# Which of the first four blocks is convolved on TensorE, and on which queue the third block is loaded: a fused causal convolution and GELU feed-forward kernel

## The chip, the cores and the metric

The kernel runs on one core of a Trainium2 chip. The metric is the device time of one execution in microseconds; the time before is the median of seven executions. A core has TensorE (PE in the profile; its weight loads are PEld), VectorE (DVE), ScalarE (ACT), GpSimd (POOL) and SyncE (SP). SP, ACT and POOL can start DMAs. Those of SP and ACT go through hardware queues, those of POOL through a software ring.

## The reference

The input x has 8 sequences of 4096 tokens with 192 channels, in 8 heads of 24. Each head has seven weights, normalised by a softmax. A token's channel becomes the weighted sum of the same channel in this token and the six before it (zeros ahead of the sequence). Then comes a feed-forward layer.

```python
w = softmax(weight)                            # (8 heads, 7 taps)
x_pad = concatenate([zeros(B, 6, D), x], axis=1)
y[b, s, h, g] = sum_k w[h, k] * x_pad[b, s + k, h, g]
h = y.reshape(B * S, 192) @ w_in               # (32768, 2048)
g = 0.5 * h * (1 + erf(h / sqrt(2)))
out = g @ w_out                                # (32768, 192), float32
```

## The kernel before

The 32768 tokens are two halves that lie side by side on the partitions (64 channels of the first half on partitions 0 to 63, of the second on 64 to 127). Each half is cut into 34 blocks (`WS`): four of 256 tokens, blocks 0 to 3, then thirty of 512. The 192 channels are three groups of 64 (`NP = 3`, index `p`).

A block n goes through these stages:

- **Load** (`load`, L172 to L185): four DMAs into `xin[n % 3]`. Block 0 is shared by SP and ACT, block 1 by SP and POOL, all others are loaded by SP.
- **Transpose** (`trans`, L371, VectorE): 32x32 blocks from `xin` to `xT[n % 2]`, float32, channels on partitions. A tap of the convolution is then a shift by 32 columns; GpSimd fills in the columns that lie ahead of the block (`halo`, L253).
- **Convolution**, in one of two ways. Blocks with n < `ND` = 3: `xT` is cast to bf16 (`cast` on VectorE, for block 0 on ScalarE), TensorE multiplies by diagonal matrices of the taps (`pconv`, L537; 14 matmuls for each p) into a part of the output accumulators `ob`, and VectorE (`conv_out`, L366) or for block 0 ScalarE copies the result to `xc[n % 2]`. All later blocks: 21 VectorE operations (`conv`, L392; seven taps by three groups) accumulate in float32 and write `xc[n % 2]`.
- **First product** (`mm1`, L575): slices into the two buffers `hp`, eight slices for a block of 256 tokens, sixteen for one of 512. ScalarE applies GELU to a slice and writes `gT[n % 2]`.
- **Second product** (`mm2`, L603): for 128 tokens of each half (a group g; two or four groups in a block) 32 units of two matmuls, 16 in each of two phases that accumulate in the same bank, into `ob[group number % 2]`. TensorE does the second product of block n - 1 between the slices of the first product of block n: the units are dealt out to the slices (L643 to L656).
- **Eviction and store** (`evac`, L418; `store`): VectorE copies a group from `ob` to `osb`, and SP stores it.

Every engine works through its list in the order in which it is written, and semaphores carry the dependences. Three orders were written by hand:

- **VectorE** (L437 to L474): blocks 0 to 2 one by one. Then for each block from 3 on the 24 operations `ops0` (three transposes, 21 taps); between them, at the positions of the table `late`, the evictions. `(2, 1): (4, 23)` says that group 1 of block 2 is evicted ahead of operation 23 of block 4, its last tap.
- **TensorE**: `behind` (L570) puts the convolution parts of the next block behind slices of the present one: those of block 1 behind slices 2, 4, 6 of block 0, those of block 2 behind slices 1, 2, 3 of block 1. The units of block 0 are spread evenly over slices 2 to 7 of block 1, those of later blocks evenly over all slices.
- **Queues**: POOL issues W_in in three pieces (`win_in`), half of block 1's load, and W_out (L290; bf16 in the kernel, converted by the DMA). SP loads block 2 after the third piece of W_in has landed, block 3 after W_out has landed, and block 4 after block 3 has landed.

Of the kernel before, what the change touches and what calls it, by code (L numbers as in the profile page):

```python
# [11 lines left out]
def bass_lightweight_conv__then__act_gelu_exact_kernel(  # L12
# [21 lines left out]
    ND = 3  # L34
# [54 lines left out]
    with es:  # L89
# [15 lines left out]
        xTb = [sbt("xTb%d" % i, [128, NP * XB], BF16) for i in range(ND)]  # L105
# [12 lines left out]
        S_XG = sem("S_XG")  # L118
# [9 lines left out]
        S_CAST = [sem("S_CAST%d" % i) for i in range(ND)]  # L128
# [15 lines left out]
        CONVB = [  # L144
            [(ob[0], 0), (ob[0], 512), (ob[1], 0)],
            [(ob[0], 0), (ob[0], 512), (ob[1], 0)],
            [(ob[1], 0), (ob[1], 512), (ob[1], 256)],
        ]
# [6 lines left out]
        def cvd(n):  # L155

            return NCV * max(0, n - ND + 1)


        HC = [0]  # L160
        for n in range(NB):
            HC.append(HC[n] + (1 + NP if n < ND else 2))

# [4 lines left out]
        def xin_at(n):  # L168

            return 64 * (n // NX + 1) - (32 if n % NX == 1 else 0)  # L170
# [58 lines left out]
        def _(g):  # L229
# [21 lines left out]
            load(g, 1, (2, 3), S_XG)  # L251

            def halo(n):  # L253

                t, tw = (xTb[n], XB) if n < ND else (xT[n % 2], XW)
                dst = ap(t, 0, [[NP * tw, 128], [tw, NP], [32, HB]])
                if n >= ND + 2:
                    g.wait_ge(S_CV, cvd(n - 2))
                elif n >= 2:
                    g.wait_ge(S_PCE, NP * (n - 1))  # L260
# [12 lines left out]
                if n < ND:  # L273
                    for p in range(NP):
                        g.wait_ge(S_TR, NP * n + p + 1)
                        g.tensor_copy(  # L276
                            ap(t, p * tw + 1, [[NP * tw, 128], [32, HB], [1, 31]]),
                            ap(xT[n % 2], p * XW + WS[n], [[NP * XW, 128], [32, HB], [1, 31]]),
                        ).then_inc(S_HALO)
                    return  # L280
# [8 lines left out]
            win_in(FP[2], FP[3], S_WIN[2])  # L289
            g.dma_start(  # L290
# [7 lines left out]
        def _(v):  # L298
# [58 lines left out]
            def cast(n, p):  # L357
                v.wait_ge(S_TR, NP * n + p + 1)
                v.tensor_copy(  # L359
                    ap(xTb[n], p * XB + HL, [[NP * XB, 128], [1, WS[n]]]),  # L360
                    ap(xT[n % 2], p * XW + HL, [[NP * XW, 128], [1, WS[n]]]),
                ).then_inc(S_CAST[n])

            def conv_out(n, p):
                v.wait_ge(S_PC, NP * n + p + 1)
                b, o = CONVB[n][p]  # L366
                v.tensor_copy(  # L367
                    xc[n % 2][:, p * TB : p * TB + WS[n]], ap(b, o, [[1024, 128], [1, WS[n]]])
                ).then_inc(S_PCE)

            def trans(n, p):  # L371
                w = WS[n]
                if p == 0:
                    v.wait_ge(S_XIN[n % NX], xin_at(n))
                    if n == 1:
                        v.wait_ge(S_XG, 32)
                    if n >= ND + 2:
                        v.wait_ge(S_CV, cvd(n - 2))
                    elif n >= 2:
                        v.wait_ge(S_PCE, NP * (n - 1))  # L380
                    if n >= 1:
                        v.wait_ge(S_HALO, HC[n])
# [65 lines left out]
            dup(2)  # L448
            for p in range(NP):
                conv_out(1, p)  # L450
            for p in range(NP):
                trans(2, p)
            for p in range(NP):
                cast(2, p)
            for p in range(NP):
                conv_out(2, p)


            late = {(0, 0): (3, 9), (0, 1): (3, 16), (1, 0): (4, 1), (1, 1): (4, 9)}
            late.update({(2, 0): (4, 16), (2, 1): (4, 23), (3, 0): (5, 14), (3, 1): (6, 1)})  # L460
# [6 lines left out]
            order = sorted(late, key=lambda k: (late[k], k))  # L467
            for b in range(ND, NB):
                for o, op in enumerate(ops0):
                    while order and late[order[0]] <= (b, o):  # L470
                        evac(*order.pop(0))
                    run(b, op)
            for k in order:
                evac(*k)  # L474
# [57 lines left out]
        def _(t):  # L532
# [4 lines left out]
            def pconv(n, p, k):  # L537
# [3 lines left out]
                if k == KS - 1:  # L541
                    t.wait_ge(S_CAST[n], p + 1)
                    if n == 0:
                        t.wait_ge(S_DG, p + 1)
                    elif n == 2 and p == 0:
                        t.wait_ge(S_PCE, 2 * NP)
                    elif n == 2 and p == 2:
                        t.wait_ge(S_PCE, 2 * NP + 1)
                if k == KS - 2:
                    t.wait_ge(S_HALO, HC[n] + 2 + p)  # L550
                for hf in range(2):
# [6 lines left out]
                        xTb[n][r, x0 : x0 + w],  # L558
# [12 lines left out]
            for p in range(NP):  # L571
                for n, i in ((1, 2 + 2 * p), (2, 1 + p)):
                    behind[n - 1, i] = [(n, p, k) for k in range(KS - 1, -1, -1)]

            def mm1(n, i):  # L575
# [4 lines left out]
                if i == 0:  # L580
                    if n < ND:
                        t.wait_ge(S_PCE, NP * (n + 1))
# [20 lines left out]
            def mm2(m, g, ph, i):  # L603
# [4 lines left out]
                if i == 0:  # L608
                    if ph == 0:
                        if gg >= 2:  # L610
                            t.wait_ge(S_EV, gg - 1)
                        elif gg == 1:
                            t.wait_ge(S_PCE, NP * ND)
# [23 lines left out]

            def units(m):
# [4 lines left out]
            for n in range(NB):  # L643
                todo = units(n - 1) if n >= 1 else []
                for i in range(NSL[n]):
# [3 lines left out]

                    i0 = 2 if n == 1 else 0  # L650
                    a0 = len(todo) * max(0, i - i0) // (NSL[n] - i0)
                    a1 = len(todo) * max(0, i + 1 - i0) // (NSL[n] - i0)
                    if n == 1 and i == i0:
# [11 lines left out]
        def _(sp):  # L665
# [45 lines left out]
```

## Time and profile before

| | |
|---|---|
| median of 7 executions | 698.77 us (697.17 to 700.78) |
| the profiled execution: its own time | 699.72 us |
| the profiled execution: span of its trace | 697.7 us |
| TensorE busy | 687.5 us (99%) |
| VectorE busy | 553.2 us (79%) |
| ScalarE busy | 528.9 us (76%) |
| GpSimd busy | 40.8 us (6%) |
| mean granted TensorE clock | 0.996 |
| time from issue to landing: W_out | 12.5 us |
| the same, three of block 2's four DMAs (issued from 14 us on), median | 5.9 us |

The span runs from the first to the last instruction of the trace; the execution's own time also holds what lies around it, 2.0 us here. A time in the profile counts from the start of the span. A busy time is a sum over the whole span; whether an engine sets the pace in one stretch is read from what the others wait for there. In a line of a timeline the first number is the start, the second the length from the first to the end of the last of the merged instructions, and the bracket at the end is the idle time just before, with what ended it. The ends of matmuls are modelled and overlap the start of the next by some 0.2 us.

### The profile page before, as it was taken

How to read it: one execution, taken by the hardware profiler on the slowest of the kernel's cores; microseconds unless marked ns; L12 is line 12 of the kernel's file. 1: busy time of each engine (PE TensorE's matmuls, PEld its weight loads, DVE VectorE, ACT ScalarE, POOL GpSimd, SP SyncE). 2: the span in 40 equal slices, each digit the busy share in tenths (PEclk: the TensorE clock that was granted, in tenths of full speed). 3: DMA queues.
4: the chain of work that ended last, by engine and by line, in shares of the span. 5: the costliest groups of instructions: out<-in, count | busy, mean ns of one | idle time of the engine just before them, and what ended most of it. 6: DMA issues, size and time to landing. Idle time of an engine off the chain costs nothing.

```text
span 697.7 us, 25349 instructions
## 1 busy us (share of the span) xinstructions
PE 687.5 (99%) x11598; PEld 529.0 (76%) x11598; DVE 553.2 (79%) x915; ACT 528.9 (76%) x524; POOL 40.8 (6%) x89
## 2 busy tenths in 40 slices
PE   8899999999999999999999999999999999999997
PEld 5687777777777777777777777777777777777777
DVE  6499977898887897888897888897887898887811
ACT  6578877777777777777777777777777777777771
POOL 5100000000000000000000000000000000000000
PEclk9999999999999999999999999999999999999999
DMA  9768433455534455443455533455533455521013
GB/s 180 179 148 192 114 77 85 116 136 137 125 74 99 115 136 137 114 102 82 115 137 137 126 91 82 113 138 136 133 86 79 114 137 137 130 53 28 22 47 93
DMA packets 23083, 78.15 MB, mean 112 GB/s; under 512 B 6977, under 2 KB 11201, under 8 KB 19137
## 3 DMA queue, kind: packets, MB, share of 16 engines
q1 hardware_dynamic: 18832, 73.80, 44.5%
q0 software_dynamic: 3408, 1.96, 2.0%
q8 instruction: 91, 1.49, 1.0%
q10 hardware_dynamic: 736, 0.78, 0.4%
q14 instruction: 16, 0.12, 0.1%
HBM read 52.92 MB, written 25.17 MB: 112 GB/s over the span
## 4 chain that ended last, share of the span: by engine, by line
PE 94%; DVE 2%; DMA 2%; issue 0%; POOL 0%; SPq 0%; ACT 0%; DVEq 0%
PE ob L627 48%; PE hp L593 45%; DMA xin<-in_x_dram 2%; DVE acc L413 1%; DMA win<-in_moe_w_in_dram 1%; PE ob L555 1%; DVE xT L383 0%; DVE xc L413 0%; DVE acc L406 0%; POOL xTb L276 0%; SPq L178 0%; DVE osb L422 0%; ACT L479 0%; POOL win L232 0%; DVE xTb L359 0%
## 5 line engine op out<-in xcount | busy, mean ns | idle before, releaser
L522 ACT ACTIVATE gT<-hp 128x1024 bf16<-128x1024 f32 x512 | 523.3, 1024 | 150.3 <-PE hp L593 150.3
L627 PEld LDWEIGHTS ob<-wout,gT 64*128 64x128 bf16 x8192 | 368.7, 94 | 99.8 <-issue 1.1
L627 PE MATMUL ob<-wout,gT 64*128 64x192 bf16 x8192 | 428.6, 243 | 0.7 <-issue 0.6
L593 PE MATMUL hp<-xc,win 64*128 64x512 bf16 (+1 forms) x3264 | 423.8, 364 | 3.3 <-DVE xc L413 1.6
L413 DVE SCALAR_TENSOR_TENSOR acc<-xT,wcol,acc 128x512 f32<-128x512 f32 (+1 forms) x465 | 311.1, 731 | 0.0
L593 PEld LDWEIGHTS hp<-xc,win 64*128 64x128 bf16 x3264 | 166.4, 94 | 56.6 <-ACT gT L522 3.4
L422 DVE COPY osb<-ob 128x384 f32<-128x384 f32 x128 | 70.3, 549 | 125.8 <-PE ob L627 125.8
L383 DVE STREAM_TRANSPOSE xT<-xin 128x512 f32<-128x512 f32 (+1 forms) x102 | 61.2, 649 | 3.0 <-DMA xin<-in_x_dram 2.8
L413 DVE SCALAR_TENSOR_TENSOR xc<-xT,wcol,acc 128x512 bf16<-128x512 f32 (+1 forms) x93 | 63.3, 732 | 0.0
L282 POOL COPY xT<-xT 128x558 f32<-128x558 f32 x31 | 20.3, 654 | 591.4 <-DVE xT L383 591.4
L406 DVE TENSOR_SCALAR acc<-xT,wcol 128x512 f32<-128x512 f32 (+1 forms) x93 | 54.0, 633 | 1.1
L265 POOL COPY xT<-xT 128x18 f32<-128x18 f32 x28 | 11.2, 399 | 0.0
L555 PE MATMUL ob<-xTb,dg 64*64 64x256 bf16 x126 | 9.1, 292 | 1.3 <-DVE xTb L359 1.3
L555 PEld LDWEIGHTS ob<-xTb,dg 64*64 64x64 bf16 x126 | 6.8, 115 | 3.5 <-DVE xTb L359 1.8
L367 DVE CAST xc<-ob 128x256 bf16<-128x256 f32 x6 | 2.5, 421 | 8.8 <-PE ob L555 8.8
L535 PE MATMUL hp<-warm 128*128 128x512 bf16 x16 | 6.3, 578 | 1.3 <-DVE warm L299 1.3
L535 PEld LDWEIGHTS hp<-warm 128*128 128x128 bf16 x16 | 2.1, 139 | 4.9 <-issue 3.5
L344 DVE COPY win<-win 64x768 bf16<-64x768 bf16 (+1 forms) x6 | 4.1, 680 | 0.3
L276 POOL CAST xTb<-xT 128x186 bf16<-128x186 f32 x9 | 3.4, 386 | 11.3 <-DVE xT L383 11.3
L232 POOL DMA_DIRECT2D win<-in_moe_w_in_dram x6 | 3.9, 659 | 0.8 <-POOLq L696 0.8
L493 ACT ACTIVATE xTb<-xT 128x256 bf16<-128x256 f32 x3 | 1.1, 417 | 2.7 <-DVE xT L383 2.7
L501 ACT ACTIVATE xc<-ob 128x256 bf16<-128x256 f32 x3 | 1.2, 384 | 1.2 <-PE ob L555 1.2
(28 smaller groups left out, 14.0 us busy)
## 6 DMA issues: line engine op xcount, KB each, us to landing
xin<-in_x_dram SPq DMA_DIRECT2D x120, 380.0 KB, 6.7
out_dram<-osb SPq DMA_DIRECT2D x116, 192.0 KB, 3.1
xin<-in_x_dram SPq DMA_DIRECT2D x12, 188.0 KB, 3.9
out_dram<-osb SPq DMA_DIRECT2D x40, 48.0 KB, 1.9
wout<-in_moe_w_out_dram POOLq DMA_DIRECT2D x1, 768.0 KB, 12.5
win<-in_moe_w_in_dram POOLq DMA_DIRECT2D x4, 96.0 KB, 4.6
win<-in_moe_w_in_dram POOLq DMA_DIRECT2D x2, 192.0 KB, 4.5
out_dram<-osb ACTq DMA_DIRECT2D x8, 48.0 KB, 2.1
```

Of the source, the lines that this page charges most:

```text
L265: g.tensor_copy(dst, ap(xT[(n - 1) % 2], WS[n - 1] + 31, [[NP * XW, 128], [XW, NP], [32, HB]],),).then_inc(S_HALO)
L282: g.tensor_copy(ap(t, 1, [[NP * tw, 128], [tw, NP], [32, HB], [1, 31]]), ap(t, WS[n], [[NP * tw, 128], [tw, NP], [32, HB], [1, 31]]),).the ...
L344: v.tensor_copy(ap(win, 64 * (1 - hf) * NP * F + FH + FP[s], [[NP * F, 64], [F, NP], [1, FP[s + 1] - FP[s]]],), ap(win, 64 * hf * NP * F + ...
L383: v.transpose(ap(xT[n % 2], p * XW + HL, [[NP * XW, 128], [1, w]]), ap(xin[n % NX], 64 * p, [[TB // 32 * D, 128], [D, w // 32], [1, 32]],) ...
L406: ins = v.tensor_scalar(a, src, wk, None, ALU.mult)
L413: ins = v.scalar_tensor_tensor(dst, src, wk, a, op0=ALU.mult, op1=ALU.add)
L422: v.tensor_copy(ap(osb[m % 2], g * C, [[8 * C, 128], [4 * C, 2], [1, C]]), ap(ob[(G0[m] + g) % 2], 0, [[1024, 128], [512, 2], [1, C]]),).t ...
L522: a.activation(out=ap(gT[n % 2], i * c * 2 * w, dst), in_=ap(hp[u % 2], 0, src), func=AF.Gelu,).then_inc(S_GELU)
L535: t.matmul(hp[1][:, 0:512], warm[:, 0:128], warm[:, :])
L555: ins = t.matmul(b[r, o : o + w], dg[r, d0 : d0 + 64], xTb[n][r, x0 : x0 + w], start=(k == KS - 1), stop=(k == 0), tile_position=(64 * hf, ...
L593: ins = t.matmul(hp[u % 2][:, hf * TB + cc * w : hf * TB + cc * w + w], win[r, p * F + wcols(hf, f0) : p * F + wcols(hf, f0) + 128], xc[n ...
L627: ins = t.matmul(ob[gg % 2][:, 512 * sub : 512 * sub + C], gT[m % 2][r, c0 : c0 + 128], wout[r, CH[i] * C : (CH[i] + 1) * C], start=(ph == ...
```

## The change

Blocks 0, 1 and 3 are now the ones that are convolved on TensorE; the table `PC` gives the number of their bf16 tile, and `pce(n, p)` the count of `S_PCE` at which part p of block n is in `xc`. Block 2 goes through VectorE's 21 taps.

Block 2's load is issued by POOL, all four DMAs, behind the third piece of W_in and ahead of W_out, and has its own semaphore `S_XG[1]`. SP no longer loads block 2 and no longer waits for block 3's landing ahead of block 4.

VectorE's hand-written order now starts its 24 operations with block 2 and skips block 3, whose transposes, casts and conv_outs become entries of one list `side` with the evictions: block 1's conv_outs stand ahead of operations 1, 4 and 8 of block 2, block 3's transposes and casts ahead of block 4, its conv_outs ahead of operations 5, 7 and 9 of block 4. The evictions of blocks 0 to 3 have new places.

On TensorE the parts of block 3 stand behind slices 1, 2, 3 of block 2, in `ob[1]`. The units of block 0 are dealt to the slices of block 1 as 0, 0, 0, 11, 11, 10, 16, 16 and those of block 1 to block 2's as 7, 7, 6, 6, 6, 11, 11, 10.

```diff
     WS = [256] * 4 + [512] * ((HALF - 1024) // 512)
-    ND = 3
+    PC = {0: 0, 1: 1, 3: 2}
     NB = len(WS)
     OFF = [sum(WS[:n]) for n in range(NB)]
     assert sum(WS) == HALF
...
         block = es.enter_context(nc.Block())
-        CONVB = [
-            [(ob[0], 0), (ob[0], 512), (ob[1], 0)],
-            [(ob[0], 0), (ob[0], 512), (ob[1], 0)],
-            [(ob[1], 0), (ob[1], 512), (ob[1], 256)],
-        ]
+        CONVB = {
+            0: [(ob[0], 0), (ob[0], 512), (ob[1], 0)],
+            1: [(ob[0], 0), (ob[0], 512), (ob[1], 0)],
+            3: [(ob[1], 0), (ob[1], 512), (ob[1], 256)],
+        }
         NCV = NP * KS
         FQ = F // 8
...
         def cvd(n):
-            return NCV * max(0, n - ND + 1)
+            return NCV * sum(m not in PC for m in range(n + 1))
+
+        def pce(n, p):
+
+            return NP * PC[n] + p + 1
         HC = [0]
         for n in range(NB):
-            HC.append(HC[n] + (1 + NP if n < ND else 2))
+            HC.append(HC[n] + (1 + NP if n in PC else 2))
         def wcols(hf, f):
...
         def xin_at(n):
-            return 64 * (n // NX + 1) - (32 if n % NX == 1 else 0)
+            return 64 * (n // NX + 1) - (0, 32, 64)[n % NX]
         def load(e, n, qs=(0, 2, 1, 3), sm=None):
             mb = WS[n] // 32
...
                     channel_multiplier=1,
                 ).then_inc(S_IDN)
             win_in(FP[1], FP[2], S_WIN[1])
-            load(g, 1, (2, 3), S_XG)
+            load(g, 1, (2, 3), S_XG[0])
             def halo(n):
-                t, tw = (xTb[n], XB) if n < ND else (xT[n % 2], XW)
+                t, tw = (xTb[PC[n]], XB) if n in PC else (xT[n % 2], XW)
                 dst = ap(t, 0, [[NP * tw, 128], [tw, NP], [32, HB]])
-                if n >= ND + 2:
-                    g.wait_ge(S_CV, cvd(n - 2))
-                elif n >= 2:
-                    g.wait_ge(S_PCE, NP * (n - 1))
+                if n >= 2 and n not in PC:
+                    if n - 2 in PC:
+                        g.wait_ge(S_PCE, pce(n - 2, NP - 1))
+                    else:
+                        g.wait_ge(S_CV, cvd(n - 2))
                 if OFF[n] % SEQ == 0:
                     g.memset(dst, 0.0).then_inc(S_HALO)
                 else:
...
                             [[NP * XW, 128], [XW, NP], [32, HB]],
                         ),
                     ).then_inc(S_HALO)
-                if n < ND:
+                if n in PC:
                     for p in range(NP):
                         g.wait_ge(S_TR, NP * n + p + 1)
                         g.tensor_copy(
...
             g.wait_ge(S_IDN, 2)
             halo(0)
             win_in(FP[2], FP[3], S_WIN[2])
+            load(g, 2, (0, 2, 1, 3), S_XG[1])
             g.dma_start(
                 ap(wout, 0, [[NF * C, 128], [C, NF], [1, C]]),
                 ap(woutt, 0, [[C, 128], [128 * C, NF], [1, C]]),
...
             def cast(n, p):
                 v.wait_ge(S_TR, NP * n + p + 1)
                 v.tensor_copy(
-                    ap(xTb[n], p * XB + HL, [[NP * XB, 128], [1, WS[n]]]),
+                    ap(xTb[PC[n]], p * XB + HL, [[NP * XB, 128], [1, WS[n]]]),
                     ap(xT[n % 2], p * XW + HL, [[NP * XW, 128], [1, WS[n]]]),
-                ).then_inc(S_CAST[n])
+                ).then_inc(S_CAST[PC[n]])
             def conv_out(n, p):
-                v.wait_ge(S_PC, NP * n + p + 1)
+                v.wait_ge(S_PC, pce(n, p))
                 b, o = CONVB[n][p]
                 v.tensor_copy(
                     xc[n % 2][:, p * TB : p * TB + WS[n]], ap(b, o, [[1024, 128], [1, WS[n]]])
...
             def trans(n, p):
                 w = WS[n]
                 if p == 0:
-                    v.wait_ge(S_XIN[n % NX], xin_at(n))
-                    if n == 1:
-                        v.wait_ge(S_XG, 32)
-                    if n >= ND + 2:
+                    if xin_at(n) > 0:
+                        v.wait_ge(S_XIN[n % NX], xin_at(n))
+                    if n in (1, 2):
+                        v.wait_ge(S_XG[n - 1], 32 * n)
+                    if n >= 2 and n - 2 in PC:
+                        v.wait_ge(S_PCE, pce(n - 2, NP - 1))
+                    elif n >= 2:
                         v.wait_ge(S_CV, cvd(n - 2))
-                    elif n >= 2:
-                        v.wait_ge(S_PCE, NP * (n - 1))
                     if n >= 1:
                         v.wait_ge(S_HALO, HC[n])
                 v.transpose(
...
             for p in range(NP):
                 cast(1, p)
             dup(2)
+
+            side = [((2, 1), conv_out, 1, 0), ((2, 4), conv_out, 1, 1), ((2, 8), conv_out, 1, 2)]
             for p in range(NP):
-                conv_out(1, p)
+                side.append(((4, 0), trans, 3, p))
             for p in range(NP):
-                trans(2, p)
-            for p in range(NP):
-                cast(2, p)
-            for p in range(NP):
-                conv_out(2, p)
-
-
-            late = {(0, 0): (3, 9), (0, 1): (3, 16), (1, 0): (4, 1), (1, 1): (4, 9)}
-            late.update({(2, 0): (4, 16), (2, 1): (4, 23), (3, 0): (5, 14), (3, 1): (6, 1)})
+                side.append(((4, 0), cast, 3, p))
+                side.append(((4, 5 + 2 * p), conv_out, 3, p))
+            late = {(0, 0): (2, 20), (0, 1): (4, 0), (1, 0): (4, 11), (1, 1): (4, 18)}
+            late.update({(2, 0): (4, 23), (2, 1): (5, 4), (3, 0): (5, 15), (3, 1): (6, 1)})
             for n in range(4, NB):
                 for g in range(NG[n]):
                     b, o = n + 2, len(ops0) * (g + 1) // (NG[n] - 1)
                     if g == NG[n] - 1:
                         b, o = n + 3, 0
                     late[n, g] = (b, o)
-            order = sorted(late, key=lambda k: (late[k], k))
-            for b in range(ND, NB):
+            for k in late:
+                side.append((late[k], evac, *k))
+            side.sort(key=lambda q: q[0])
+            for b in range(2, NB):
+                if b in PC:
+                    continue
                 for o, op in enumerate(ops0):
-                    while order and late[order[0]] <= (b, o):
-                        evac(*order.pop(0))
+                    while side and side[0][0] <= (b, o):
+                        side[0][1](*side[0][2:])
+                        side.pop(0)
                     run(b, op)
-            for k in order:
-                evac(*k)
+            for q in side:
+                q[1](*q[2:])
         @block.scalar
         def _(a):
...
                 w = WS[n]
                 b, o = CONVB[n][p]
                 if k == KS - 1:
-                    t.wait_ge(S_CAST[n], p + 1)
+                    t.wait_ge(S_CAST[PC[n]], p + 1)
                     if n == 0:
                         t.wait_ge(S_DG, p + 1)
-                    elif n == 2 and p == 0:
-                        t.wait_ge(S_PCE, 2 * NP)
-                    elif n == 2 and p == 2:
-                        t.wait_ge(S_PCE, 2 * NP + 1)
+                    elif n == 3 and p == 0:
+                        t.wait_ge(S_EV, G0[1])
+                    elif n == 3 and p == 2:
+                        t.wait_ge(S_PCE, pce(3, 0))
                 if k == KS - 2:
                     t.wait_ge(S_HALO, HC[n] + 2 + p)
                 for hf in range(2):
...
                     ins = t.matmul(
                         b[r, o : o + w],
                         dg[r, d0 : d0 + 64],
-                        xTb[n][r, x0 : x0 + w],
+                        xTb[PC[n]][r, x0 : x0 + w],
                         start=(k == KS - 1),
                         stop=(k == 0),
                         tile_position=(64 * hf, 64 * hf),
...
             behind = {}
             for p in range(NP):
-                for n, i in ((1, 2 + 2 * p), (2, 1 + p)):
+                for n, i in ((1, 2 + 2 * p), (3, 1 + p)):
                     behind[n - 1, i] = [(n, p, k) for k in range(KS - 1, -1, -1)]
             def mm1(n, i):
...
                 if u >= 2:
                     t.wait_ge(S_GELU, u - 1)
                 if i == 0:
-                    if n < ND:
-                        t.wait_ge(S_PCE, NP * (n + 1))
+                    if n in PC:
+                        t.wait_ge(S_PCE, pce(n, NP - 1))
                     else:
                         t.wait_ge(S_CV, cvd(n))
                 if n == 0 and i in (0, 2, 4):
...
                     if ph == 0:
                         if gg >= 2:
                             t.wait_ge(S_EV, gg - 1)
-                        elif gg == 1:
-                            t.wait_ge(S_PCE, NP * ND)
+                        if (m, g) == (1, 1):
+                            t.wait_ge(S_PCE, pce(3, NP - 1))
                     else:
                         t.wait_ge(S_PH, gg + 1)
                 if g == 0 and ph == 0:
...
                 if i == NF - 1:
                     ins.then_inc(S_MM2 if ph == 1 else S_PH)
+
+
+            share = {1: [0, 0, 0, 11, 11, 10, 16, 16], 2: [7, 7, 6, 6, 6, 11, 11, 10]}
+
             def units(m):
                 return [
                     (g, ph, i) for g in range(NG[m]) for ph in range(2) for i in range(NF)
...
                     mm1(n, i)
                     for q in behind.get((n, i), []):
                         pconv(*q)
-
-                    i0 = 2 if n == 1 else 0
-                    a0 = len(todo) * max(0, i - i0) // (NSL[n] - i0)
-                    a1 = len(todo) * max(0, i + 1 - i0) // (NSL[n] - i0)
-                    if n == 1 and i == i0:
+                    ws = share.get(n, [1] * NSL[n])
+                    a0 = len(todo) * sum(ws[:i]) // sum(ws)
+                    a1 = len(todo) * sum(ws[: i + 1]) // sum(ws)
+                    if n == 1 and a0 == 0 and a1 > 0:
                         t.wait_ge(S_WOUT, 16)
                     for un in todo[a0:a1]:
                         mm2(n - 1, *un)
...
             load(sp, 0, (0, 1))
             sp.wait_ge(S_WIN[0], 32)
             load(sp, 1, (0, 1))
-            sp.wait_ge(S_WIN[2], 32)
-            load(sp, 2)
             sp.wait_ge(S_WOUT, 16)
             load(sp, 3)
-            sp.wait_ge(S_XIN[3 % NX], xin_at(3))
             for n in range(1, NB):
                 if n + 3 < NB:
                     load(sp, n + 3)
```

More of the change, by code (lines that the diff above doesn't have):

```diff
@@ L104, in bass_lightweight_conv__then__act_gelu_exact_kernel @@
         hot = sbt("hot", [1, 2], F32)
-        xTb = [sbt("xTb%d" % i, [128, NP * XB], BF16) for i in range(ND)]
+        xTb = [sbt("xTb%d" % i, [128, NP * XB], BF16) for i in range(len(PC))]
         xin = [sbt("xin%d" % i, [128, TB // 32 * D], F32) for i in range(NX)]
@@ L117, in bass_lightweight_conv__then__act_gelu_exact_kernel @@
         S_WOUT = sem("S_WOUT")
-        S_XG = sem("S_XG")
+        S_XG = [sem("S_XG%d" % i) for i in range(2)]
         S_XIN = [sem("S_XIN%d" % i) for i in range(NX)]
@@ L127, in bass_lightweight_conv__then__act_gelu_exact_kernel @@
         S_HOT = sem("S_HOT")
-        S_CAST = [sem("S_CAST%d" % i) for i in range(ND)]
+        S_CAST = [sem("S_CAST%d" % i) for i in range(len(PC))]
         S_PC = sem("S_PC")
```

## Prediction

> **What bounds the kernel now.** I read the page first (busy shares, then the chain), then TensorE's timeline up to 78 us, then VectorE's, the chain, the stretches of 1 us with the granted clock, and the bytes of each DMA queue.
>
> ```profile
> PE 687.5 (99%) x11598; PEld 529.0 (76%) x11598; DVE 553.2 (79%) x915; ACT 528.9 (76%) x524; POOL 40.8 (6%) x89
> ```
>
> TensorE is the bound. The change leaves its 11598 matmuls as they are, so it can win or lose only where TensorE stands idle or runs slowly, and that is ahead of 77 us. TensorE's timeline (start, length, what, idle before):
>
> ```profile
> 19.17 1.51 PE L593 MATMUL hp<-xc,win 64*128 64x256 bf16 x24
> 21.12 0.83 PE L593 MATMUL hp<-xc,win 64*128 64x256 bf16 x12 [0.44 <-ACT gT L522]
> 23.30 1.33 PE L555 MATMUL ob<-xTb,dg 64*64 64x256 bf16 x14 [1.35 <-DVE xTb L359]
> 24.56 1.46 PE L593 MATMUL hp<-xc,win 64*128 64x256 bf16 x12
> 25.95 1.51 PE L555 MATMUL ob<-xTb,dg 64*64 64x256 bf16 x14
> ...
> 50.72 0.75 PE L627 MATMUL ob<-wout,gT 64*128 64x192 bf16 x14 [0.56 <-issue]
> ...
> 60.77 0.82 PE L593 MATMUL hp<-xc,win 64*128 64x512 bf16 x6 [1.40 <-DVE xc L413]
> ```
>
> See the stop before 23.30 (the convolution of block 2 waits for its cast), the stop before 60.77, and that 12 and 14 matmuls take 1.46 and 1.51 us where they elsewhere take 0.82 and 0.95. The one-microsecond stretches tell why (after the busy times: granted clock, DMA share, GB/s):
>
> ```profile
> 22.00:23.00 1.00, 0.00 (x0) 0.00 (x0) 1.00 (x4) 1.00 (x1) 0.57 (x2) 1.00 0.05 16
> 23.00:24.00 1.00, 0.70 (x11) 0.65 (x13) 0.80 (x4) 0.02 (x1) 0.66 (x3) 0.86 0.98 277
> 25.00:26.00 1.00, 1.00 (x12) 0.46 (x10) 0.09 (x1) 0.00 (x0) 0.00 (x0) 0.50 0.92 265
> 27.00:28.00 1.00, 1.00 (x24) 0.78 (x20) 0.42 (x1) 0.09 (x1) 0.00 (x0) 0.93 0.00 0
> ```
>
> The clock is halved from about 23.7 to 27.1. The stop itself starts at the load of block 2, and the later one at an eviction (chain of waits, start, length):
>
> ```profile
> 15.02 6.87 DMA xin<-in_x_dram
> ...
> 59.40 0.07 DVE osb L422
> ...
> 59.88 0.74 DVE xc L413
> ```
>
> The load lands at 21.89. At 59.38 the last matmul of block 2's second output group ends; VectorE evicts it and only then does the last tap of block 4, for which TensorE waits.
>
> **TensorE's loss before.** Unit costs from the chain where nothing waits: a slice of the first product (12 short or 6 long matmuls) 0.66 us, 8 units of the second (16 matmuls) 0.66, a convolution part (14) 0.88. From block 1's first slice (19.83) to block 5's first: 8 slices 5.3, 64 units 5.3, three parts 2.6, blocks 2 and 3 10.5 each, block 4 16 slices and 64 units 15.8: 49.9 us. It took 76.75 - 19.83 = 56.9. The 7.0 lost, from issue to issue: 0.63 and 1.52 before 21.12 and 23.30; 1.4 by the half clock; 0.6 at two accumulation hand-overs (unit 16 to 17 with no slice of the first product between); 0.56 "issue"; 1.59 and 0.17 before 60.77 and 76.75; 0.5 unnamed.
>
> **The change part by part.**
>
> *Load 2 to the software ring.* It leaves SP's queue (four DMAs, first at 13.67) and goes behind the third piece of W_in on POOL, ahead of W_out. POOL's two issues of this shape took 0.52 us each, so four are 2.1: issued from 9.6 to 11.7. Queued behind on POOL are W_out's issue (9.57 to about 11.7) and block 1's halo copies (10.76 to 12.85; their parts end at 14.1, not 13.15). Block 1's first convolution part needs the first of them at its second tap, so it ends some 0.4 later than 14.0; its cover is the wait for the last copy of W_in (mm1 starts at 15.23 after 0.38 idle), so I cost it at 0; without cover, 0.4.
>
> When does it land? The software queue's row, 7:8 and 16:17 us (packets, MB, share):
>
> ```profile
> q0 software_dynamic: 171, 0.35, 130.6%
> ...
> q0 software_dynamic: 468, 0.18, 150.3%
> q1 hardware_dynamic: 4, 0.02, 6.5%
> ```
>
> W_in's third piece leaves the ring at about 12.5 (landing 13.65). Below: 752 KB at the 350 GB/s of 7:8, when the half of block 1 on this ring went through, is 2.2, and 0.9 for the landing: 15.6. Above: the 6.87 us of before, counted from the last issue at 11.7: 18.6. Nearest is that half: begun near 6.8, landed near 9.7, 2.9 us for 376 KB; with 1.1 for as much again, 4.0. I take 16.3. Before, SP's copy moved almost nothing until 17 because W_out's small packets filled the engines (row 16:17).
>
> *What waits on it.* VectorE is free at 15.08 after the last W_in copy and now stands at block 2's transpose until 16.3. Queued behind are block 1's three conv_outs, the last at position (2,8): three transposes 1.1, three conv_outs 1.1, five taps of 0.43 and 0.40 (1.35/3, 2.85/7), 2.1, together 4.4: 20.7. TensorE's slice 0 of block 1 starts at 20.8, not 19.83. Then GELU paces it (1.0 each, two buffers): slices at 20.8, 21.5, 22.8, 23.8. The first three of them stand without second-product work, which begins behind slice 3. Loss to 23.8: 23.8 - 19.83 - 2.0 = 2.0, where before lost 2.15 and the half clock.
>
> *W_out later.* Its bytes start at about 15.2, not 12.5. Most took 5 us, the tail to 22.07. If the tail is engine time that load 2 shared, it lands near 22.3, if it is per packet, 24.5 (up to 25.4 by the 12.5 us from issue). It is needed at 24.4. I take 23.4: 0. Loads 3 and 4 follow it at once (their waits for each other are gone): 2.27 MB at 245 GB/s, landing near W_out + 4 and W_out + 11.2 = 34.6.
>
> *Block 2's taps on VectorE, block 3 on TensorE.* Taps 12 x 0.40 from 20.7, then eviction (0,0), which waits for its group (TensorE 29 us), four taps: block 2 ready at 31.2. TensorE, with 3.3 of slices and 5.3 of units from 23.8, asks at 32.7: 0, margin 1.5. VectorE then: transposes of block 3 1.1, casts 0.9, eviction (0,1) 0.5: 33.7; TensorE's first part of block 3 comes at 34.8. Transposes of block 4 from 34.6, 1.9, two taps 1.2, conv_out 0.4: 38.1, and part 3, which needs it, comes at 39.3. Last conv_out 41.5, needed at 42.5. All within 1.0 to 1.5 of each other: 0 taken, up to 1 if W_out is late.
>
> *Evictions moved.* (2,1) goes from (4,23) to (5,4), so block 4's last tap follows (2,0), which is complete halfway through block 3: ready near 53, asked at 57. The 1.59 goes. Next: eviction (2,1) at block 4's start t, 12 operations 7.2, eviction (3,0), 9 taps 6.1: t + 14.7 against t + 15.8. Margin 1.1, so the 0.17 goes too.
>
> *Shares of the second product.* 11, 11, 10, 16, 16 and 7, 7, 6, 6, 6, 11, 11, 10 put three hand-overs inside a share (0.3 each): 0.9 against 0.6; bounds 0 and 0.9.
>
> Loss after: 2.0 + 0.9 + 0.56 (issue, kept) + 0.5 (unnamed, kept) = 4.0. Gain 7.0 - 4.0 = 3.0, carried to the end, as TensorE is busy throughout from 80 us to its last matmuls. The profiled execution took 699.72 (span 697.7), 0.95 over the median of 698.77: 699.72 - 3.0 = **696.7**, 2.1 under the median.
>
> **A rule against the row.** The Trainium skill's "TensorE: Matmul & The Clock Gate", Part 1, lets the clock fall only after at least one idle window of about 3.4 us, free-running. The longest stop here is 1.5 us, yet the row shows 0.50 for 3.4 us: here about half a window idle was enough. By the rule the half clock has nothing to do with the stop and stays: gain 1.6, 698.1. By the row it goes, 696.7, but the new stops (1.0, 0.6, 0.3 between 19.8 and 23.8) come near the same half window and can bring it back. The stretch 57 to 61 with 1.4 idle stayed at 1.00. I follow the row. If the window runs free, as the page says, the median execution before may have escaped the halving, and 0.95 under the profile fits that; the time after is reckoned without it and stays.
>
> **Rivals.**
> 1. *The stop comes back as another* (no change, 0.20). For: the idle sum after is 1.9 against 2.15. Half clock costs 1.4: 698.1. W_out at 25.4 costs 1.0: 697.7. Against: clock stayed full at 1.4 idle.
> 2. *Slower: block 2's load lands late and VectorE holds block 1's finished convolution behind it* (0.14). Each us of landing past 16.3 is a us of TensorE at block 1's slice 0; from about 17 the stop is over 1.7 and halves the clock (1.4). It is over 700.17 from a landing at 18.4 on; at 18.6, 700.4, at 20, 701.8. For: 18.6 is what before's own load took. Against: W_out's packets are now behind it.
> 3. *The convolution swap does nothing and only the eviction order pays*: 1.76 of gain, 698.0 from the profile; in the chance of 1.
>
> **Numbers.** My forecast 0.66. Measurement tells 0.2% (1.4 us) from no change: faster is below 697.37. Low end: landing at 15.6 (-0.7), no issue stop (-0.56), hand-overs free (-0.6): 694.9. High end, to leave out 2 in 10: 699.6, landing near 17.6 with the clock halved. Faster 0.66, same 0.20, slower 0.14.
>
> **What would show it.** Right: block 2's transpose near 16.3 released by DMA; slice 0 of block 1 near 20.8 after about 1 us, waiting for conv_out; clock 1.00 throughout 23 to 27; no stop of 1.4 before block 4; block 5's first slice near 73.7. Wrong: transpose after 18, clock 0.50 again, TensorE waiting for W_out or for block 3's conv_outs.

## The result, and the profile after

The changed kernel takes 696.09 us (median of 13 executions, 695.86 to 696.80), the kernel before in the same comparison 698.64 (32 executions, 697.17 to 701.48): ratio 0.9964, 95% interval 0.9954 to 0.9973. It is faster by 2.5 us. Forecast were 696.7 and a gain of 2.1 against the median. The profiled execution took 695.97 (span 694.0), 3.7 less than the profiled one of before (699.72), which is not a typical one: 1.1 of the 3.7 is its distance from the median of before.

TensorE does the same 11598 matmuls (after):

```profile
PE 685.1 (99%) x11598; PEld 503.5 (73%) x11598; DVE 552.6 (80%) x915; ACT 528.8 (76%) x524; POOL 43.3 (6%) x93
```

TensorE's timeline after, at block 1's first slices and at the first slices of blocks 4 and 5:

```profile
21.24 1.49 PE L602 MATMUL hp<-xc,win 64*128 64x256 bf16 x24 [0.98 <-DVE xc L373]
23.19 1.74 PE L602 MATMUL hp<-xc,win 64*128 64x256 bf16 x24 [0.46 <-ACT gT L531]
24.77 1.07 PE L636 MATMUL ob<-wout,gT 64*128 64x192 bf16 x22
...
57.48 0.81 PE L602 MATMUL hp<-xc,win 64*128 64x512 bf16 x6
...
73.12 0.81 PE L602 MATMUL hp<-xc,win 64*128 64x512 bf16 x6
```

Block 5's first slice in the profile of before:

```profile
76.75 0.82 PE L593 MATMUL hp<-xc,win 64*128 64x512 bf16 x6 [0.17 <-DVE xc L413]
```

A new stop of 0.98 us stands at 21.24 and waits for a conv_out; then GELU paces the slices; the stop of 1.40 ahead of block 4 is gone (57.48 carries no bracket), and block 5 starts at 73.12 instead of 76.75: 3.6 us of the profile's 3.7. The one-microsecond stretches after (the third number from the end is the granted clock) show the full clock where it was halved:

```profile
22.00:23.00 1.00, 0.73 (x14) 0.45 (x9) 1.00 (x4) 0.89 (x1) 0.00 (x0) 1.00 0.31 65
23.00:24.00 1.00, 0.81 (x12) 0.50 (x12) 1.00 (x4) 1.00 (x2) 0.00 (x0) 1.00 0.49 138
25.00:26.00 1.00, 1.00 (x28) 0.97 (x24) 0.85 (x3) 1.00 (x2) 0.00 (x0) 1.00 1.04 307
27.00:28.00 1.00, 1.00 (x22) 0.95 (x24) 0.00 (x0) 0.56 (x1) 0.00 (x0) 1.00 0.99 219
```

VectorE's timeline after tells who makes the new stop. The software queue's row of 13 to 14 us (packets, MB, share) is the only queue that moves data then, with packets of 4 KB in the mean; they are block 2's. Before, this queue moved 0.13 MB in that microsecond, in 335 packets, 329 of them under 512 bytes:

```profile
16.83 0.45 DVE L390 STREAM_TRANSPOSE xT<-xin 128x256 f32<-128x256 f32 x1 [1.48 <-DMA xin<-in_x_dram]
...
18.29 0.83 DVE L413 TENSOR_SCALAR acc<-xT,wcol 128x256 f32<-128x256 f32 x1
...
20.68 0.41 DVE L373 CAST xc<-ob 128x256 bf16<-128x256 f32 x1
...
52.90 0.74 DVE L420 SCALAR_TENSOR_TENSOR xc<-xT,wcol,acc 128x512 bf16<-128x512 f32 x1
```

```profile
q0 software_dynamic: 76, 0.30, 96.3%
```

Block 2 lands at 16.8, not 21.9. Block 1's last conv_out runs at 20.68, though its matmuls ended at 19.4: it stood behind block 2's transposes and taps, and TensorE behind it. Block 4's last tap is done at 53.64, long before TensorE asks for it at 57.48.

### The profile page after: what moved, and what is told of

It reads as the page before. It is cut to its first block, busy times and chain, and to the rows that moved or that the text cites. A ratio compares the mean times of both kernels' runs of the same rounds, so it can differ in the third digit from the quotient of the medians.

```text
span 694.0 us, 25348 instructions
## 1 busy us (share of the span) xinstructions
PE 685.1 (99%) x11598; PEld 503.5 (73%) x11598; DVE 552.6 (80%) x915; ACT 528.8 (76%) x524; POOL 43.3 (6%) x93
## 4 chain that ended last, share of the span: by engine, by line
PE 96%; DMA 2%; DVE 1%; POOL 1%; ACT 0%; issue 0%
PE ob L636 49%; PE hp L602 47%; DMA xin<-in_x_dram 2%; PE ob L564 0%; ACT gT L531 0%; DVE xT L390 0%; POOL xin L182 0%; DVE acc L413 0%; POOL xTb L281 0%; POOL win L236 0%; ACT L488 0%; DVE acc L420 0%; DVE xc L373 0%; DVE osb L429 0%
## 5 line engine op out<-in xcount | busy, mean ns | idle before, releaser
L636 PEld LDWEIGHTS ob<-wout,gT 64*128 64x128 bf16 x8192 | 352.4, 94 | 115.8 <-PE ob L636 0.9
L636 PE MATMUL ob<-wout,gT 64*128 64x192 bf16 x8192 | 420.5, 243 | 0.2
L602 PE MATMUL hp<-xc,win 64*128 64x512 bf16 (+1 forms) x3264 | 415.1, 363 | 3.0 <-DVE xc L373 1.0
L602 PEld LDWEIGHTS hp<-xc,win 64*128 64x128 bf16 x3264 | 150.1, 94 | 64.0 <-issue 2.6
L182 POOL DMA_DIRECT2D xin<-in_x_dram x6 | 3.0, 512 | 0.0
## 6 DMA issues: line engine op xcount, KB each, us to landing
wout<-in_moe_w_out_dram POOLq DMA_DIRECT2D x1, 768.0 KB, 10.3
```

The lines of the kernel that those rows point to most:

```text
L602: ins = t.matmul(hp[u % 2][:, hf * TB + cc * w : hf * TB + cc * w + w], win[r, p * F + wcols(hf, f0) : p * F + wcols(hf, f0) + 128], xc[n ...
L636: ins = t.matmul(ob[gg % 2][:, 512 * sub : 512 * sub + C], gT[m % 2][r, c0 : c0 + 128], wout[r, CH[i] * C : (CH[i] + 1) * C], start=(ph == ...
```

## The experiments

The experiments fall in three groups, each on another chip, with the kernel before beside them: its median is 698.75 in group 1 (35 executions), 699.59 in group 2 (10) and 698.59 in group 3 (14). The group of an experiment is given with its time. The medians of before differ by 1.0 us, mostly because a lower mean clock fell on 7 of 35, 5 of 10 and 1 of 14 of its executions: the median of the others is 698.67, 698.44 and 698.58. So the times of the variants are set against each other directly, but across groups a difference under some 0.3 us tells nothing. The ratios are against the kernel before of the same group. The changed kernel was run again in group 3 (696.25).

**The kernel before again.** No edit.

> The kernel before, unchanged, to see what its own spread is made of. Theory (the stop of 1.5 us at block 2's cast halves the clock only when it falls badly[...]): executions fall in two groups, mean granted clock near 0.996 and 1.000, the first 1.2 to 1.8 us longer; median 698.6, and the changed kernel's narrow spread (1.0 us against 4.3) comes from having no such stop. Rival (the halving is in every execution, and the spread is something else): all executions near 0.996, no relation of time to clock.

699.13 us (group 1; 12 executions, 6 of them at a mean clock of 0.998 or less). With the executions of before from the three groups there are 71: 19 at 0.998 or less, with a median of 700.2, and 52 at 0.999 or more, with a median of 698.6. So about a quarter of the executions, between 1 of 14 and half in a group, have a lower clock, and those take 1.6 us longer. The profile shown ahead of the prediction is one of these; the median is not. That each of the 19 has its clock halved at the same place is inferred: 3.4 us at half the clock take 0.0024 off the mean of 697 us, which fits 0.998, but only one of them has a profile. (Its own mean of 0.996 holds a second fall behind the last matmul, at 690 to 698 us, which costs nothing.) The profile of this run has the full clock, and a smaller stop at block 2's cast; the stop ahead of block 4 is the same:

```profile
24.03 0.95 PE L555 MATMUL ob<-xTb,dg 64*64 64x256 bf16 x14 [0.73 <-DVE xTb L359]
...
59.93 0.82 PE L593 MATMUL hp<-xc,win 64*128 64x512 bf16 x6 [1.40 <-DVE xc L413]
```

So the stop at the cast differs between executions (1.35 and 0.73), and how much of the 1.6 us is the clock and how much a longer stop was not separated.

**Only block 2's evictions moved** (on the kernel before).

```diff
-            late.update({(2, 0): (4, 16), (2, 1): (4, 23), (3, 0): (5, 14), (3, 1): (6, 1)})
+            late.update({(2, 0): (4, 23), (2, 1): (5, 4), (3, 0): (5, 14), (3, 1): (6, 1)})
```

> The kernel before with block 2's two evictions alone at the places of the changed kernel: (2,0) ahead of block 4's last tap, (2,1) ahead of block 5's second tap. Theory (the 1.59 us stop ahead of block 4 comes from the eviction's place): the stop falls to about 0.3 (VectorE no longer waits 0.6 at (2,0), but is still late by its own work), gain 1.3 to 1.5 us, 697.2. Rival (VectorE was late because block 3's taps were its work, and only the swap of the blocks helps): the stop stays above 1.0, gain below 0.6.

698.89 us (group 1), ratio 0.9998 (0.9989 to 1.0008): nothing gained. TensorE's timeline:

```profile
36.91 0.83 PE L627 MATMUL ob<-wout,gT 64*128 64x192 bf16 x16 [0.72 <-DVE osb L422]
...
58.28 0.82 PE L593 MATMUL hp<-xc,win 64*128 64x512 bf16 x6 [0.81 <-DVE xc L413]
...
74.72 0.82 PE L593 MATMUL hp<-xc,win 64*128 64x512 bf16 x6 [0.63 <-DVE xc L413]
```

The stop ahead of block 4 fell from 1.40 to 0.81, the one ahead of block 5 rose from 0.17 to 0.63: VectorE is late for other reasons in its list, and the moved evictions only shift where that shows. The theory's 0.3 is refuted. Further up VectorE stands 1.81 us at eviction (1,0), which was not moved:

```profile
41.73 0.56 DVE L422 COPY osb<-ob 128x384 f32<-128x384 f32 x1 [1.81 <-PE ob L627]
```

**Only block 2's load moved** (on the kernel before: the four DMAs to the software ring ahead of W_out, with their semaphore, as in the change).

```diff
             win_in(FP[2], FP[3], S_WIN[2])
+            load(g, 2, (0, 2, 1, 3), S_XG[1])
...
-            sp.wait_ge(S_WIN[2], 32)
-            load(sp, 2)
```

> The kernel before with block 2's load alone moved to the software ring ahead of W_out; blocks 0 to 2 still on TensorE, evictions as before, block 4's load still behind block 3's landing. Theory: block 2 lands near 16.8, its cast is done near 21.8, ahead of TensorE's question (about 21.8), so the stop at 23.30 and the half clock go; the stop of about 1.6 ahead of block 4 stays. First slice of block 4 near 57.8 instead of 60.77 in the profile, gain against the median 1.5 to 3.0 us, 695.6 to 697.1. Rival (the early load is worth something only together with block 2's taps on VectorE): VectorE is behind by then and gain is under 0.7.

697.14 us (group 1), ratio 0.9980 (0.9968 to 0.9991): 1.6 us gained, with no part of the swap. There is no stop at block 2's cast in its profile, all clocks are 0.999 or more, and the 1.40 ahead of block 4 stays:

```profile
22.39 0.95 PE L557 MATMUL ob<-xTb,dg 64*64 64x256 bf16 x14
...
59.45 0.82 PE L595 MATMUL hp<-xc,win 64*128 64x512 bf16 x6 [1.40 <-DVE xc L415]
```

Block 4 starts at 59.45 there and not near 57.8: the profiled execution is the slowest of the twelve (698.34), with two more stops of 0.75 and 0.79 us.

**Both edits, no swap** (the early load, and block 2's two evictions moved).

> Both edits together on the kernel before, without the swap of blocks 2 and 3 between VectorE and TensorE. Theory (the load and the eviction order are the whole gain, and the swap costs by putting block 1's conv_outs behind block 2's transposes, 1.1 us, and by slices without second-product work): 694.5 to 695.3, 0.8 to 1.6 faster than the changed kernel. Rival (the swap is a part of the gain): 696.0 or more.

696.65 us (group 1), ratio 0.9973 (0.9964 to 0.9982). That is 0.5 less than with the load alone, with intervals that overlap, and 0.4 to 0.6 slower than the changed kernel: as the rival said, and 1.4 above the theory's range. VectorE's timeline names the time that it lost:

```profile
39.07 0.70 DVE L385 STREAM_TRANSPOSE xT<-xin 128x512 f32<-128x512 f32 x1
42.60 0.56 DVE L424 COPY osb<-ob 128x384 f32<-128x384 f32 x1 [2.83 <-PE ob L629]
```

It stands 2.83 us at the eviction (1,0), which the hand-written order puts ahead of operation 1 of block 4, before its group is complete. This profile is again the slowest of its twelve (698.71), and TensorE itself had stopped just before; the GELU named as releaser had ended 0.7 us before that stop did:

```profile
37.78 0.84 PE L629 MATMUL ob<-wout,gT 64*128 64x192 bf16 x16 [1.74 <-ACT gT L524]
```

That made the group late; in the profiles with one of the two edits alone the wait at (1,0) is 1.8 us, in the one of before 0.92. The changed kernel has that eviction at (4,11).

**The early load, and all evictions late; no swap.**

```diff
-            late = {(0, 0): (3, 9), (0, 1): (3, 16), (1, 0): (4, 1), (1, 1): (4, 9)}
-            late.update({(2, 0): (4, 16), (2, 1): (4, 23), (3, 0): (5, 14), (3, 1): (6, 1)})
+            late = {(0, 0): (3, 9), (0, 1): (3, 18), (1, 0): (4, 6), (1, 1): (4, 13)}
+            late.update({(2, 0): (4, 23), (2, 1): (5, 4), (3, 0): (5, 14), (3, 1): (6, 1)})
```

> The kernel before with the early load and the evictions of blocks 0 to 2 all placed where their groups are complete: (0,1) at (3,18), (1,0) at (4,6), (1,1) at (4,13), (2,0) at (4,23), (2,1) at (5,4); no swap. With the early load and only block 2's evictions moved VectorE stood 2.8 us at eviction (1,0), and TensorE stopped 0.8 and 0.6 us ahead of blocks 4 and 5. Theory A (VectorE is late only because it stands at evictions written too early): both stops go, 694.5 to 695.6, as fast as the changed kernel or faster. Theory B (VectorE is late because it idles before 28 us, where only the swap gives it work): one stop of over 0.5 us stays, 696.0 to 696.7.

695.07 us (694.87 to 696.12; group 2), ratio 0.9940 (0.9920 to 0.9959): 4.5 below the median of before beside it, half of whose executions had the lower clock, and 3.4 below the others (698.44). It is some 1.0 below the changed kernel, which was not run beside it. TensorE's timeline at block 2's convolution and at blocks 4 and 5 has no stop of VectorE's making:

```profile
22.55 0.95 PE L557 MATMUL ob<-xTb,dg 64*64 64x256 bf16 x14
...
56.15 0.81 PE L595 MATMUL hp<-xc,win 64*128 64x512 bf16 x6
...
72.02 0.82 PE L595 MATMUL hp<-xc,win 64*128 64x512 bf16 x6
```

VectorE does not stand at the evictions (1,0), (1,1) and (2,0) either:

```profile
42.03 0.55 DVE L424 COPY osb<-ob 128x384 f32<-128x384 f32 x1
...
47.14 0.55 DVE L424 COPY osb<-ob 128x384 f32<-128x384 f32 x1
...
54.23 0.55 DVE L424 COPY osb<-ob 128x384 f32<-128x384 f32 x1
```

Theory A held: VectorE was late because it stood at evictions written too early, not because its work was too much for it.

**All evictions late, the load as before.**

> The kernel before with the five evictions at their late places, but block 2's load still on SP. Theory (two separate stops: the eviction places cost VectorE, the late load costs TensorE near 22 us): the stops ahead of blocks 4 and 5 go, the stop at block 2's cast and now and then the half clock stay; 1.2 to 2.2 below the kernel before beside it. Rival (the early load is what gives VectorE its slack): a stop of 0.5 or more stays ahead of block 4, gain under 0.7.

696.67 us (group 3), ratio 0.9973 (0.9963 to 0.9982): 1.9 gained. The stops ahead of blocks 4 and 5 are gone, the one at block 2's cast is there, and one of nine executions has a clock of 0.998:

```profile
23.28 0.95 PE L555 MATMUL ob<-xTb,dg 64*64 64x256 bf16 x14 [1.25 <-DVE xTb L359]
...
56.98 0.83 PE L593 MATMUL hp<-xc,win 64*128 64x512 bf16 x6
...
72.75 0.82 PE L593 MATMUL hp<-xc,win 64*128 64x512 bf16 x6
```

Load alone 1.6 and evictions alone 1.9 make 3.5; both together gave 3.4 against executions of before with the full clock, 4.5 against all ten beside it. The three gains come from three chips, so that they add is shown only to within this 1 us; that each pays without the other is shown.

**The changed kernel with the load put back on SP.**

```diff
-            load(g, 2, (0, 2, 1, 3), S_XG[1])
...
+            sp.wait_ge(S_WIN[2], 32)
+            load(sp, 2, sm=S_XG[1])
```

> The changed kernel, with block 2's load put back on SP after the third piece of W_in, as before the change; everything else of the change stays. Theory (the order of the work on VectorE is only good with the early load): block 2 lands near 21.9 instead of 16.8, slice 0 of block 1 moves from 21.2 to about 26.3, the stop halves the clock (1.5 us), 701.5 to 702.8. Rival (VectorE has slack enough and the swap alone is faster than before): below 698.7.

702.43 us (group 2), ratio 1.0045 (1.0027 to 1.0063): slower than before, inside the theory's range. VectorE's timeline, TensorE's, and a stretch with the clock:

```profile
22.22 0.45 DVE L389 STREAM_TRANSPOSE xT<-xin 128x256 f32<-128x256 f32 x1 [7.11 <-DMA xin<-in_x_dram]
```

```profile
26.64 4.92 PE L601 MATMUL hp<-xc,win 64*128 64x256 bf16 x48 [6.61 <-DVE xc L372]
```

```profile
27.00:28.00 1.00, 1.00 (x14) 0.81 (x10) 1.00 (x4) 0.00 (x0) 0.00 (x0) 0.50 0.96 225
```

Block 2's transpose runs at 22.22 instead of 16.83, 5.4 us later; slice 0 of block 1 comes 5.4 us later, at 26.64; all six executions have a clock of 0.993 to 0.995, and the time is 6.3 longer. This is the mechanism of the prediction's second rival (the slower one), at its price of one us for each us of landing; 0.9 is left for the clock, where that rival had 1.4.

**The changed kernel with block 1's conv_outs earlier.**

```diff
-            side = [((2, 1), conv_out, 1, 0), ((2, 4), conv_out, 1, 1), ((2, 8), conv_out, 1, 2)]
+            side = [((2, 0), conv_out, 1, 0), ((2, 0), conv_out, 1, 1), ((2, 6), conv_out, 1, 2)]
```

> The changed kernel with block 1's conv_outs earlier in VectorE's order: two ahead of block 2's transposes, the third ahead of operation 6. Theory (the stop of 1.0 us at block 1's slice 0 is VectorE holding block 1's finished convolution behind block 2's late load): slice 0 at about 20.1 instead of 21.24, GELU then paces, 0.4 to 0.8 us less, 695.3 to 695.7. Rival (GELU and the first slices without second-product work set the time anyway): less than 0.2 gained.

695.74 us (695.24 to 696.90; group 2): 0.35 gained against the changed kernel's 696.09, which is at the limit of what can be told across groups. The stop at slice 0 falls to 0.40, at 20.57, but its profile (696.90, the slowest of the five) has a stop without a releaser later:

```profile
20.57 1.55 PE L602 MATMUL hp<-xc,win 64*128 64x256 bf16 x24 [0.40 <-DVE xc L373]
...
36.89 0.67 PE L636 MATMUL ob<-wout,gT 64*128 64x192 bf16 x12 [1.53 <-issue]
```

**The changed kernel with shares cut at the phases.**

```diff
-            share = {1: [0, 0, 0, 11, 11, 10, 16, 16], 2: [7, 7, 6, 6, 6, 11, 11, 10]}
+            share = {1: [0, 0, 0, 8, 8, 16, 16, 16], 2: [8, 8, 5, 5, 6, 8, 8, 16]}
```

> The changed kernel with the second product's shares cut at its phases: 0,0,0,8,8,16,16,16 and 8,8,5,5,6,8,8,16. Theory (each hand-over inside a share costs 0.3 us): three fewer but one, 0.6 to 0.9 us less, 695.2 to 695.5. Rival (a hand-over's time is taken from the wait that follows, VectorE's or GELU's): under 0.2.

696.00 us (695.17 to 696.05; group 2): 0.1 gained, which is nothing that can be told. Its profile:

```profile
22.00 1.49 PE L602 MATMUL hp<-xc,win 64*128 64x256 bf16 x24 [1.52 <-DVE xc L373]
23.94 1.75 PE L602 MATMUL hp<-xc,win 64*128 64x256 bf16 x24 [0.46 <-ACT gT L531]
...
73.07 0.81 PE L602 MATMUL hp<-xc,win 64*128 64x512 bf16 x6
```

Slice 0 of block 1 starts at 22.00, because block 2 landed at 17.6, and block 5 at 73.07: 51.1 us between them against 51.9 in the changed kernel's (73.12 - 21.24) and 51.8 in that of its second run below. So the profile shows the 0.8 for the three hand-overs and a landing that took it back; the median of five does not settle it. It shows one thing more: stops of 1.52 and 0.46, larger than those that came ahead of the half clock before (1.35 and 0.44), and the clock of this execution is 1.000.

**The changed kernel again.**

> The changed kernel, unchanged, beside the two that may beat it, and for its spread: 695.9 to 696.3, all clocks 0.999 or more.

696.25 us (695.89 to 696.58; group 3), all clocks 1.000.

**Both last edits on the changed kernel.**

> The changed kernel with block 1's conv_outs early and the shares cut at the phases, together. If the two add (0.5 and 0.6): 694.9 to 695.3. If a stop called issue near 35 us takes it back, as in the one profile with conv_outs early alone: 695.7 or more.

695.12 us (694.49 to 696.42; group 3), 1.1 below the changed kernel beside it, in spite of a stop of 0.53 near 35 us in its profile. That is the sum of the 0.5 and 0.6 expected; the two alone had measured 0.35 and 0.1 on another chip, so the pair is shown to pay, and how it is shared between them is not.

**Early load, late evictions, and shares of block 0 cut at the phases; no swap.** The share code is the change's, with `{1: [0, 0, 8, 8, 8, 8, 16, 16]}`.

> The kernel before with the early load, the five late evictions, and block 0's second product in shares 0,0,8,8,8,8,16,16; no swap. Theory (both hand-overs inside a share go, 0.3 each): 694.3 to 694.8, the fastest, 1.3 to 1.8 under the changed kernel. Rival (VectorE is then late, or TensorE meets another stop): 695.0 or more.

695.40 us (694.13 to 695.56; group 3): above the theory's range, 0.85 below the changed kernel beside it, and not told apart from the 695.07 without the shares. Its profile's W_in copy ended late (the slice that needs it starts at 16.37 instead of 15.89), and 0.27 went to "issue".

So three kernels beat both the changed kernel and the kernel before: the change with early conv_outs and cut shares (695.12), and the kernel before with the early load and late evictions, with cut shares (695.40) and without (695.07). Their differences are within their spreads.

## Why the prediction was right, point by point

- **The load.** Landing was put at 16.3 (15.6 to 18.6); the transpose ran at 16.83, 17.42 and 17.58 in three profiles. Right in kind, 0.5 to 1.3 early in size; the working's own 12.5 and 4.0 make 16.5. The row of block 1's half, from which the 4.0 was taken, was a good base. The load is worth 1.6 by itself.
- **What waits on it.** Slice 0 was forecast at 20.8, behind a conv_out, and came at 21.24; the first slice with second-product work at 23.8, and came at 24.10 in the chain. The loss up to there was 2.3, not 2.0: the landing. VectorE's part from the transpose to the end of the last conv_out took 4.26 against 4.4, and the landings of 17.42 and 17.58 moved slice 0 by as much (21.82 and 22.00). But the stops were smaller than the second rival reckoned, 1.04 and 1.52 and not over 1.7, because block 0's last slices were late too in these executions, and they did not halve the clock.
- **The clock.** The prediction followed the row and not the full idle window of the Trainium skill's "TensorE: Matmul & The Clock Gate", Part 1, and that was right: in the profile of before it is halved after stops of 1.35 and 0.44 us, 19 of 71 executions have a lower clock, and the changed kernel's 18 never do (0.999 or more in all). But a stop of that size does not always halve it: 1.52 and 0.46 in the profile with cut shares, and 1.74 at 37.78 in the one with both edits, passed at a clock of 1.000 and 0.999. A window that runs free, as that page has it, would make it depend on where a stop falls; no run shows the window. So that the new stops brought no half clock was in part luck. That the median of before escapes it was right. Set against executions with the full clock, the gain is the same 2.5.
- **"The 1.59 goes", put down to the eviction (2,1).** It went, and block 4's last tap was ready at 53.64, near the 53 reckoned. But the cause was named too narrowly: with block 2's two evictions moved alone nothing was gained. Without the swap the stop goes when the evictions from (0,1) on come late as well. In the changed kernel all of them are late and the blocks are swapped, and no run separates the two there. That the term of 1.59 came true is so in part luck. Rival 3, with its 698.0 for the eviction order, had the wrong edit (698.89) and, with the right one, was too small (696.67).
- **The swap.** I took it at the stops that it brings and at no gain of its own. Load and evictions without it are 1.0 faster (0.85 on the same chip, there with cut shares), so in this form it costs about 1. With the conv_outs ahead and the shares cut, this is gone.
- **W_out.** Landing was put at 23.4; 10.3 us after its issue at 11.61, against 12.5 before, it landed near 21.9. The margin was larger than reckoned, and rival 1's 1.0 us did not come.

```profile
wout<-in_moe_w_out_dram POOLq DMA_DIRECT2D x1, 768.0 KB, 10.3
```

- **0.56 "issue" kept.** The largest mis-sized term: it does not occur in the changed kernel's two profiles. The sum without it and with the later landing is 7.0 - (2.3 + 0.9 + 0.5) = 3.3, against 3.6 measured at block 5. The forecast was 0.6 too slow, and this term and the landing, 0.3 the other way, make half of that; the rest has no name.

## What to carry to other kernels

A stop that a profile puts down to one operation may have been made by waits further up in the same engine's list: sum the idle brackets of that engine first, and move all waits that come before their data is ready and ahead of work that another engine will soon want. (The changed kernel's VectorE still stands 3.32 us at eviction (0,0), and loses nothing by it: block 2 is ready at 31.3, and TensorE comes to it at 32.9.) Whenever a late load is moved, look at what stands behind its first consumer in that engine's order: here one transpose held back finished work for TensorE. And a single profile can be of the less frequent kind; the clock of many executions tells which.

## What the runs showed that I had not expected

- **The first VectorE multiply of a block takes longer, beside a GpSimd copy.** The first tap of block 2 in the changed kernel took 0.83 us, each of the next two 0.34 (0.60 together, as they overlap); a GpSimd copy into `xT` ran beside the first:

```profile
18.32 0.65 POOL L287 COPY xT<-xT 128x558 f32<-128x558 f32 x1 [3.88 <-DVE xT L390]
```

```profile
19.37 0.60 DVE L413 TENSOR_SCALAR acc<-xT,wcol 128x256 f32<-128x256 f32 x2
...
55.48 0.96 DVE L413 TENSOR_SCALAR acc<-xT,wcol 128x512 f32<-128x512 f32 x1
...
58.16 0.87 DVE L413 TENSOR_SCALAR acc<-xT,wcol 128x512 f32<-128x512 f32 x2
```

  At 512 columns the first takes 0.96 and each of the next two 0.48 (0.87 together), and a copy of the same shape runs beside the first again. The extra is some 0.49 both times. The means used in the sum (0.45) had mixed the two kinds. In these profiles that copy always starts with the first tap, which is also the first one behind the transposes, so that the copy is the cause is not shown.
- **Stops called "issue" on TensorE.** 0.56 in both profiles of before, 0.27 to 1.74 in six of the edited kernels', none in the others, at places between 35 and 51 us; some are given a releaser (an eviction, a GELU), but that had ended 0.35 to 0.8 us before the stop did. They may explain a part of each kernel's spread of 1 to 2 us. What they wait for stays open; late instructions would fit, and no run tried it.
